# A recurrence, a routed feed-forward layer and a mish layer on one core: another PSUM bank for k's rows, weights loaded in parts, alpha's range checked elsewhere

## The chip, the core and the metric

The kernel runs on one core of a Trainium2 chip. Its time is the device time of one execution in microseconds (us); the number compared is the median of several executions. The engines are named as in the profile: PE (matrix multiply), PEld (its weight load), DVE (vector), ACT (activation), POOL (general purpose), SP (which here only issues DMAs). PE's clock has two levels, 1.2 and 2.4 GHz; the profile gives the granted clock as a share of the upper one, so 0.50 is the lower level all the time.

## The reference, cut to what matters

Four sequences (B = 4) of 8 heads, 768 steps and 48 columns go through a gated linear recurrence; its output, 3072 tokens of 384, goes to one of 8 experts each, and then through a dense layer with the mish function:

```python
for t in range(S):                                   # recurrence, per batch and head
    state = alpha[:, :, t, :, None] * state + np.einsum('bhd,bhe->bhde', k[:, :, t], v[:, :, t])
    y[:, :, t] = np.einsum('bhd,bhde->bhe', q[:, :, t], state)
expert_idx = np.argmax(x @ w_gate, axis=1)           # router: one expert a token
out[mask] = gate_w[mask, None] * (np.maximum(x[mask] @ w1[e], 0.0) @ w2[e])
g = h * np.tanh(np.log1p(np.exp(np.minimum(h, 20.0))))   # h = x @ w_in
return g @ w_out
```

## The kernel before, in words

The program is one order of instructions for each engine, written out by hand. It has three stages.

**Recurrence and routing.** A sequence of 768 steps is cut into 6 chunks of 128. Heads are taken in pairs (16 pairs in all), and two pairs make a round. One *unit* is one chunk of two pairs; there are 48 (`UNITS`). `run` (line 275) walks over them. In unit u it issues `scores(u+1)` (PE products of k and q into the PSUM tile `sc`, masked by DVE on line 223), `state(u)` (line 245, the chunk's contribution to the state, then DVE line 250 and ACT line 252), some of the setup, `rows_of_k(u+1)` (PE transposes on line 232 into `kps`, copied by ACT on line 234 into `kn`, which `state(u+1)` needs), the router's `step(2u)`, loads of v, more setup, `step(2u+1)`, and `result(u)` (line 264 and 269 into the PSUM tile `y`, copied by ACT on line 272). `kps` is the upper half of `y`'s first bank (line 82). `result` leaves a closure behind in `now`; the next `step(2u)` runs it: it turns y back into rows with PE (line 481, into the PSUM tile `xps`) and copies them with ACT (line 484).

**Setup** prepares k and q for a round of two pairs: PE transposes alpha, k and q (`columns`, line 118, PSUM tile `tp` with two buffers), ACT copies alpha's columns (lines 135 and 136), DVE scans them backward and forward (lines 152 and 169) and multiplies (line 181). `top` (line 138) checks alpha's range with two ACT passes over its rows, and only then loads the next alpha into the same tile. The first round is set up by halves of 384 steps, all later ones whole. The setup steps are in a list `todo`, each with a weight; `upto` runs them when they are due: the first 30 by unit 5, the rest by unit `READY` = 35. `busy` issues PE products of zeros to no purpose but to keep PE at work: 20 ahead of the first scores, 40 in units 1 and 3.

**Routing** (`Router`) makes each token's expert and place in small steps in a list `later`; below `SINGLE` = 76 half-units one of them runs per unit, after that several. `quick` (line 655) turns the range check into a flag.

**Experts** (lines 971 to 1006), with PE at work throughout, and beside them `fills`: DVE and ACT steps that narrow 64-bit weights to 32 bits, spread evenly over 116 slots. The weights of expert 0 come by two 1.5 MB DMAs on ACT's queue at half-unit 62, expert 1's first by one at 86; `pieces(0)` splits them from half-unit 72 on. **The mish layer** follows.

Of the kernel before, what the change touches and what calls it, by code (L numbers as in the profile page):

```python
# [21 lines left out]
P = 128  # L22
# [7 lines left out]
UNITS, READY = B * NC * NP // 2, 35  # L30

WARM_FIRST = 20
WARM, WARM_UNITS = 40, (1, 3)


class Attention:


    def __init__(self, ctx, early, late, tc, q, k, v, alpha, ident, warm, emit_y, place):
# [19 lines left out]
        self.rows = [tiles[:2], tiles[4:6], tiles[6:]]  # L59
        for n in range(2):  # L60
            for i in range(3):
                (nc.gpsimd if n else nc.vector).memset(self.rows[i][n][:, :, :, D:], 0.0 if i else 1.0)

# [8 lines left out]
        self.most = setup.tile([P, 1], F32, name="most")  # L72
        nc.gpsimd.memset(self.most, -A_MAX)
# [8 lines left out]
        self.kps = self.y[:, 0, 2 * P:].rearrange("p (j t) -> p j t", j=2)[:, :, :112]  # L82
        self.xps = ps_c.tile([P, 2, P], F32, name="xps")
# [10 lines left out]
        self.over = c.tile([P, 2, B * NP], F32, name="over")  # L94
# [6 lines left out]
    def load(self, i, n):  # L101

        if n < B * NP:
            t, b, hp = self.rows[i][n % 2], n // NP, n % NP
            for h in range(2):
                self.nc.sync.dma_start(out=t[:, :, h, :D],  # L106
                                       in_=self.src[i][b, 2 * hp + h].rearrange("(c p) d -> p c d", p=P))
# [7 lines left out]
    def columns(self, i, n, half):  # L115
        ps = self.ps_t.tile([P, 3, P], F32, name="tp")
        for j in range(3):
            self.nc.tensor.transpose(  # L118
                ps[:112, j], self.rows[i][n % 2][:, 3 * half + j].rearrange("p h d -> p (h d)")[:, :112], self.ident)
        if half and i:  # L120
            self.load(i, n + 2)
        return ps[:112]

    def alpha(self, n, half):
# [6 lines left out]
        if n == 0 and half:  # L131
            nc.vector.tensor_copy(to[:, :, 1:], ps[:, :, 1:])
            nc.vector.tensor_copy(self.a0[:, n % 2, cs], ps[:, :, 0])
        else:
            nc.scalar.activation(out=to[:, :, 1:], in_=ps[:, :, 1:], func=AF.Copy)  # L135
            nc.scalar.activation(out=self.a0[:, n % 2, cs], in_=ps[:, :, 0], func=AF.Copy)
# [48 lines left out]
    def setup(self):  # L185

        A = lambda n: [(0.3, lambda z=z: self.alpha(n, z)) for z in range(2)]
        top = lambda n: [(0.2, lambda: self.top(n))]
# [4 lines left out]
        lo, hi = (0, 384), (384, S)  # L193
        first = [*A(0), *back(0, *lo), *A(1), *back(1, *lo), *mid(0, 0, 3), *scale(1, 0, 0), *forth(0, *lo),
                 *scale(2, 0, 0), *forth(1, *lo), *scale(1, 1, 0), *scale(2, 1, 0)]
        rest = [*back(0, *hi), *back(1, *hi), *mid(0, 3, NC), *forth(0, *hi), *scale(1, 0, 1), *top(0),
                *scale(2, 0, 1), *forth(1, *hi), *scale(1, 1, 1), *top(1), *scale(2, 1, 1)]
        for p in range(2, B * NP, 2):
            q = p + 1
            rest += [*A(p), *back(p), *top(p), *A(q), *back(q), *top(q), *mid(p), *forth(p), *scale(1, p),  # L200
                     *forth(q), *scale(2, p), *scale(1, q), *scale(2, q)]
# [24 lines left out]
    def rows_of_k(self, u):  # L226
        nc = self.nc
        b, c, z, ns, t = self.pairs(u)
        if c < NC - 1:
            ps = self.kps  # L230
            for j, n in enumerate(ns):
                nc.tensor.transpose(ps[:, j], self.kh[n][:, t], self.ident[:112, :112])
            self.kn[u] = kn = self.wk.tile([P, 2, P], F32, name="kn")
            nc.scalar.activation(out=kn[:, :, :112], in_=ps, func=AF.Copy)
# [40 lines left out]
    def run(self, step):  # L275
# [5 lines left out]
        early, late = sum(w for w, _ in self.todo[:30]), sum(w for w, _ in self.todo[30:])  # L281
        due = lambda u: early * (u + 1) / 5 if u < 5 else early + late * (u - 4) / (READY - 5)
# [20 lines left out]
        for i in range(3):  # L303
            self.load(i, 0)
            self.load(i, 1)
        self.load_v(0)
        self.load_v(1)
        for n, (_, f) in enumerate(first):
            f()
            if n == 6:  # L310
                step(-4)
        loaded = 2
        self.busy(WARM_FIRST)
        scores(0)
        self.rows_of_k(0)
        for u in range(UNITS):
            if u + 1 < UNITS:
# [5 lines left out]
            step(2 * u)  # L323
# [9 lines left out]
            step(2 * u, True)  # L333
            step(2 * u + 1, True)
# [77 lines left out]
class Router:  # L412
# [14 lines left out]
    def setup(self, att, w_gate):  # L427
# [11 lines left out]
        self.bad = cst.tile([P, 2], BF16, name="bad")  # L439
        self.limits = cst.tile([1, NE + 2], F32, name="limits")  # L440
# [33 lines left out]
    def emit_y(self, b, c, z, yt):  # L474
# [157 lines left out]

    def step(self, second):

        if second:
            self.put(True)
            return
        if self.later:
            self.later.pop(0)()
        while self.now:  # L640
# [775 lines left out]
```

## Time and profile before

| | us |
|---|---|
| median of 3 runs | 927.88 (923.14 to 929.74) |
| profiled execution, its own time | 931.71 |
| its span, first to last instruction | 930.0 |
| PE / PEld / DVE / ACT / POOL busy in the span | 868.6 / 806.8 / 637.6 / 600.7 / 106.7 |

The profile is one execution. Busy time is summed over the span; a PE that is busy can still run at the lower clock, so a stage has to be read with the granted clock beside it. A wait is named by the waiting engine, its tile and line, and then by what released it; idle time of an engine off the path that sets the end costs nothing.

### The profile page before, as it was taken

What the parts mean: (1) busy time and instruction counts of PE and PEld (TensorE: products, weight loads), DVE (VectorE), ACT (ScalarE), POOL (GpSimd) and SP (SyncE); (2) the same over time, 40 slices, a digit from 0 to 9 for tenths busy, and PEclk for the clock granted to TensorE, in tenths of its full rate; (3) what the DMA queues carried; (4) which work ended last, traced back from release to release, by engine and by line L of the source; (5) the groups of instructions that cost most, each with busy time, mean ns of one, the idle gap of its engine ahead of it and who ended that gap; (6) DMA issues with size and microseconds to landing.
All of it is one profiled execution on the core that took longest, in us unless ns stands there. A gap on an engine that the chain in (4) does not pass through costs nothing.

```text
span 930.0 us, 15412 instructions
## 1 busy us (share of the span) xinstructions
PE 868.6 (93%) x5696; PEld 806.8 (87%) x5697; DVE 637.6 (69%) x1369; ACT 600.7 (65%) x1325; POOL 106.7 (11%) x162
## 2 busy tenths in 40 slices
PE   6889888798989999999999999999999999999993
PEld 4667666566779999999999899999999999999993
DVE  5556767455347877677663897868697777768682
ACT  1544565344335655455445998979797988889891
POOL 3000030204033101111003001010100101010101
PEclk8797999785589999999999999999999999999997
DMA  9843697662226667775652200000000000000000
GB/s 134 125 80 66 114 133 131 83 201 61 85 53 201 219 199 210 223 234 185 219 191 70 69 1 26 1 26 1 18 9 1 26 1 26 1 26 1 26 1 30
DMA packets 136877, 81.53 MB, mean 88 GB/s; under 512 B 111200, under 2 KB 126818, under 8 KB 136792
## 3 DMA queue, kind: packets, MB, share of 16 engines
q1 hardware_dynamic: 126632, 63.68, 28.9%
q0 software_dynamic: 4352, 9.41, 3.2%
q10 hardware_dynamic: 5808, 7.35, 2.5%
q8 instruction: 47, 0.77, 0.4%
q14 instruction: 38, 0.31, 0.1%
HBM read 66.79 MB, written 14.37 MB: 87 GB/s over the span
## 4 chain that ended last, share of the span: by engine, by line
PE 77%; issue 9%; ACT 5%; DVE 3%; DMA 3%; POOL 1%; SPq 1%; another core or an unknown queue 1%; POOLq 0%; ACTq 0%; DVEq 0%
PE o L1101 19%; PE hps L1057 19%; PE hps L981 12%; PE yps L1001 12%; PE tp L118 3%; PE y L264 2%; PE sc L220 2%; PE y L269 2%; ACT out L142 1%; PE xps L481 1%; SPq L106 1%; ACT at L135 1%; PE xtp L958 1%; ACT t L252 1%; POOL ids_dram L366 1%
## 5 line engine op out<-in xcount | busy, mean ns | idle before, releaser
L981 PE MATMUL hps<-xt,h 128*128 128x432 f32 x384 | 107.6, 358 | 0.0
L1064 DVE TENSOR_SCALAR u<-u 128x384 f32<-128x384 f32 x128 | 46.2, 361 | 83.1 <-ACT u L1063 80.2
L1071 ACT ACTIVATE r<-v,one 128x384 f32<-128x384 f32 x128 | 79.1, 618 | 4.2
L1072 ACT ACTIVATE r<-r,ln 128x384 f32<-128x384 f32 x128 | 79.0, 617 | 4.2
L981 PEld LDWEIGHTS hps<-xt,h 128*128 128x128 f32 x384 | 72.2, 188 | 3.4 <-ACT xt L968 0.2
L1080 DVE SCALAR_TENSOR_TENSOR u<-u,hps 128x384 f32<-128x384 f32 x128 | 70.9, 554 | 4.4
L923 DVE TENSOR_TENSOR l<-raw,h 128x512 fp32r<-128x512 f32 x96 | 64.8, 683 | 11.3 <-ACT h L921 11.3
L1063 ACT ACTIVATE u<-hps 128x384 f32<-128x384 f32 x128 | 61.2, 478 | 17.4 <-PE hps L1057 16.9
L1088 DVE TENSOR_TENSOR gl<-u,gh 128x384 fp32r<-128x384 f32 x128 | 70.6, 551 | 0.7 <-ACT gh L1084 0.6
L1077 DVE SCALAR_TENSOR_TENSOR u<-v,r 128x384 f32<-128x384 f32 x128 | 70.6, 551 | 0.0
L1079 DVE SCALAR_TENSOR_TENSOR u<-u,r 128x384 f32<-128x384 f32 x128 | 70.5, 551 | 0.0
L981 PE MATMUL hps<-xt,l 128*128 128x432 f32 x192 | 69.2, 361 | 0.0
L1001 PE MATMUL yps<-hh,h 128*128 128x432 f32 x192 | 69.1, 360 | 0.0
L1001 PE MATMUL yps<-hh,l 128*128 128x432 f32 x192 | 68.5, 357 | 0.0
L1001 PE MATMUL yps<-hlo,h 128*128 128x432 f32 x192 | 68.5, 357 | 0.0
L366 POOL DMA_INDIRECT out_dram<-xg,ix x24 | 23.4, 977 | 387.3 <-ACT xg L1115 382.4
L1070 ACT ACTIVATE v<-u 128x384 f32<-128x384 f32 x128 | 66.9, 522 | 1.6 <-DVE u L1064 0.2
L1084 ACT ACTIVATE gh<-u 128x384 fp32r<-128x384 f32 x128 | 65.8, 514 | 1.8 <-DVE u L1080 1.8
L1057 PE MATMUL hps<-x2h,winh 128*128 128x384 f32 x192 | 64.8, 337 | 2.0 <-DVE u L1080 2.0
L1101 PE MATMUL o<-raw,gh 128*128 128x384 f32 x192 | 65.2, 340 | 0.0
L1057 PE MATMUL hps<-x2h,winl 128*128 128x384 f32 x192 | 65.2, 340 | 0.0
L1101 PE MATMUL o<-h,gh 128*128 128x384 f32 x192 | 65.1, 339 | 0.0
(198 smaller groups left out, 2214.0 us busy)
## 6 DMA issues: line engine op xcount, KB each, us to landing
raw<-in_moe_w_dram SPq DMA_DIRECT2D x12, 1536.0 KB
raw<-in_moe_w_dram ACTq DMA_DIRECT2D x4, 1536.0 KB
f<-in_moe_w_out_dram SPq DMA_DIRECT2D x16, 384.0 KB
f<-in_moe_w_in_dram SPq DMA_DIRECT2D x10, 512.0 KB
h<-in_alpha_dram SPq DMA_DIRECT2D x32, 144.0 KB
l<-in_k_dram SPq DMA_DIRECT2D x32, 144.0 KB
l<-in_q_dram SPq DMA_DIRECT2D x32, 144.0 KB
vt<-in_v_dram SPq DMA_DIRECT2D x32, 144.0 KB
```

The source lines that it names most:

```text
L981: nc.tensor.matmul(ps, lhsT=a[:, k, f * P:f * P + P], rhs=x[:, k], start=n == 0, stop=n == 8)
L1001: nc.tensor.matmul(ps, lhsT=a[:, f, k * P:k * P + P], rhs=h[:, f], start=n == 0, stop=n == 23)
L1057: nc.tensor.matmul(ps, lhsT=a[:, k, fs], rhs=x[:, k], start=n == 0, stop=n == 8)
L1070: nc.scalar.activation(out=v, in_=self.u[g], func=AF.Square)
L1071: nc.scalar.activation(out=r, in_=v, func=AF.Ln, bias=self.one)
L1072: nc.scalar.activation(out=r, in_=r, func=AF.Exp, scale=-1.0, bias=self.ln2)
L1077: op(out=u, in0=v, scalar=1.0, in1=r, op0=ALU.add, op1=ALU.mult)
L1079: op(out=u, in0=u, scalar=4.0, in1=r, op0=ALU.subtract, op1=ALU.mult)
L1080: op(out=u, in0=u, scalar=2.0, in1=h, op0=ALU.add, op1=ALU.mult)
L1084: self.nc.scalar.activation(out=self.gg[g][0], in_=self.u[g], func=AF.Copy)
L1088: self.nc.vector.tensor_sub(gl, self.u.pop(g), gh.bitcast(F32))
L1101: nc.tensor.matmul(self.acc[i], lhsT=a[:, t], rhs=w, start=f == 0 and n == 0, stop=f == 15 and n == 2)
```

## The change

- `kps` moves from `y`'s bank to the bank of `xps` (one tile of four quarters). The copy of `kps` is split off as `keep_k`, and the order becomes: transposes of k, PE products of the way back into `xps`, ACT copy of `kps`, ACT copy of `xps`.
- `step(2u)` moves to the head of the unit, ahead of `scores(u+1)`; the way back no longer runs in it.
- `top` goes. Alpha gets four row tiles in place of two, and the next alpha is loaded as soon as PE has transposed the old one. A new class `Range` reads alpha a second time beside the experts: 18 DMAs of 128 x 512, 18 DVE maxima, and one small product at the end.
- Rounds 1 and 2 (pairs 2 to 5) are set up by halves too, and the halves are interleaved. The first 11 steps of `todo` are due by unit 2, the rest by unit 36.
- `busy(20)` stands ahead of the last two steps of the first half round; five times 20 in units 0 to 4 take the place of twice 40.
- k's first loads go on ACT's queue. Expert 0's weights come in 10 parts on SP's queue from half-unit 56 on, one a half-unit; expert 1's first in 6 parts from 82 on.
- Four zero fills of `xg` move from POOL at the start to ACT at half-units 76 to 79; the splitting of expert 0's weights starts at 74.

```diff
-UNITS, READY = B * NC * NP // 2, 35
+UNITS, READY = B * NC * NP // 2, 36
-WARM, WARM_UNITS = 40, (1, 3)
+WARM, WARM_UNITS = 20, range(5)
...
-        self.rows = [tiles[:2], tiles[4:6], tiles[6:]]
+        self.rows = [tiles[:4], tiles[4:6], tiles[6:]]
...
-        self.kps = self.y[:, 0, 2 * P:].rearrange("p (j t) -> p j t", j=2)[:, :, :112]
-        self.xps = ps_c.tile([P, 2, P], F32, name="xps")
+        out = ps_c.tile([P, 4, P], F32, name="xps")
+        self.xps, self.kps = out[:, :2], out[:, 2:, :112]
...
-        if half and i:
-            self.load(i, n + 2)
+        if half:
+            self.load(i, n + len(self.rows[i]))
...
-    def top(self, n):
-        for z in range(2):
-            t = self.wk.tile([P, NC * 2, D], F32, name="out", bufs=1)
-            self.nc.scalar.activation(out=t, in_=self.rows[0][n % 2].rearrange("p c h d -> p (c h) d")[:, :, :D],
-                                      func=AF.Relu, scale=1.0 - 2 * z, bias=self.most,
-                                      accum_out=self.over[:, z, n:n + 1])
-        self.load(0, n + 2)
...
+        first, rest = half(0, 0), half(0, 1)
+        first.insert(9, (0.0, lambda: self.busy(WARM_FIRST)))
+        for p in (2, 4):
+            rest += [*half(p, 0), *half(p, 1)]
...
-        early, late = sum(w for w, _ in self.todo[:30]), sum(w for w, _ in self.todo[30:])
-        due = lambda u: early * (u + 1) / 5 if u < 5 else early + late * (u - 4) / (READY - 5)
+        early, late = sum(w for w, _ in self.todo[:11]), sum(w for w, _ in self.todo[11:])
+        due = lambda u: early * (u + 1) / 2 if u < 2 else early + late * (u - 1) / (READY - 2)
...
-            self.load(i, 0)
-            self.load(i, 1)
+            for n in range(2):
+                self.load(i, n, self.nc.scalar if i == 1 else None)
...
         for u in range(UNITS):
+            step(2 * u)
             if u + 1 < UNITS:
                 scores(u + 1)
             self.state(u)
             upto(u + 0.3)
             if u + 1 < UNITS:
                 self.rows_of_k(u + 1)
-            step(2 * u)
+            back(lambda: u + 1 < UNITS and self.keep_k(u + 1))
...
-        def back():
+        def back(between):
             for j in range(2):
                 nc.tensor.matmul(ps[:, j], lhsT=yt[:, j], rhs=self.back[:, 2 * z + j], start=True, stop=True)
+            between()
...
+        def load(n):
+            self.rows[n] = t = self.p.tile([P, self.w], F32, name="alpha")
+            self.nc.sync.dma_start(out=t, in_=self.src[:, n * self.w:n * self.w + self.w])
+
+        def look(n):
+            self.nc.vector.tensor_reduce(out=self.most[:, n:n + 1], in_=self.rows.pop(n), op=ALU.max,
+                                         axis=mybir.AxisListType.X, apply_absolute_value=True)
...
-            if i == 62:
-                ex.load(0, 0, nc.scalar)
-                ex.load(0, 1, nc.scalar)
-            if i == 72:
+            if i == 56:
+                loads.extend(ex.load_parts(0, 0))
+                loads.extend(ex.load_parts(0, 1, 4))
+            if loads:
+                loads.pop(0)()
+            if i == 74:
...
-            if i == 86:
-                ex.load(1, 0, nc.scalar)
+            if i == 82:
+                loads.extend(ex.load_parts(1, 0))
...
+        rg = Range(words, tc, alpha)
+        for n, f in enumerate(rg.steps()):
+            fills.insert(3 + 4 * n, f)
```

## Rows read from the trace of the kernel before

**Rows 1.** Windows: stretch and length (us), busy per engine (count), clock, DMA share, GB/s
```profile
5.00:15.00 10.00, 4.68 (x29) 3.58 (x28) 7.62 (x15) 1.54 (x6) 4.97 (x39) 0.82 1.49 169
16.80:47.40 30.60, 25.30 (x245) 20.61 (x244) 18.56 (x32) 13.95 (x43) 0.00 (x0) 0.75 0.77 120
66.00:80.00 14.00, 14.00 (x95) 11.22 (x91) 6.99 (x14) 3.23 (x10) 0.00 (x0) 0.51 0.28 55
80.00:171.00 91.00, 78.09 (x898) 60.74 (x898) 66.50 (x133) 49.59 (x161) 11.89 (x21) 1.00 0.69 115
171.00:192.40 21.40, 15.20 (x105) 11.60 (x103) 9.43 (x18) 11.11 (x34) 3.56 (x4) 0.60 0.77 162
207.00:253.50 46.50, 40.74 (x305) 31.49 (x305) 21.38 (x89) 17.01 (x52) 12.08 (x17) 0.53 0.29 79
274.70:508.30 233.60, 233.60 (x1238) 223.71 (x1237) 161.01 (x299) 124.98 (x245) 38.99 (x36) 1.00 0.62 194
```

**Rows 2.** Windows of line 223 alone, one a unit: DVE busy (count), clock, DMA
```profile
66.00:80.00 14.00, 1.38 (x2) 0.51 0.28 55
80.00:171.00 91.00, 13.71 (x20) 1.00 0.69 115
207.00:253.50 46.50, 5.51 (x8) 0.53 0.29 79
```

**Rows 3.** Waits of PE, 0 to 275 us: total us, times, longest us
```profile
PE y L264 <- ACT kn L234: 22.6, 19, 5.7
...
PE tp L118 <- DMA h<-in_alpha_dram: 2.2, 2, 1.8
...
PE tp L118 <- ACT out L142: 1.5, 1, 1.5
...
PE route L536 <- DVE new L250: 0.8, 2, 0.6
```

**Rows 4.** Waits of PE, 80 to 171 us
```profile
PE y L264 <- ACT kn L234: 10.9, 11, 1.3
```

**Rows 5.** Waits of PE, 47.4 to 66 us
```profile
PE y L264 <- ACT kn L234: 3.1, 3, 1.6
```

**Rows 6.** Timeline inside one unit: start, us, engine, line, tiles, idle before
```profile
104.17 0.36 PE L232 MATMUL y<-ident,kh 112*128 112x112 f32 x2
...
105.46 0.37 ACT L234 ACTIVATE kn<-y 128x224 f32<-128x224 f32 x1
...
105.70 0.40 ACT L484 ACTIVATE x<-xps 128x240 f32<-128x240 f32 x1
...
105.89 0.65 PE L264 MATMUL y<-st,vt 128*64 128x128 f32 x8 [0.91 <-ACT kn L234]
```

**Rows 7.** Groups by line, 0 to 270 us: busy us, mean ns, idle before
```profile
L142 ACT ACTIVATE out<-h,most 128x576 f32<-128x576 f32 x32 | 24.7, 771 | 0.5
```

**Rows 8.** Timeline of the start
```profile
3.11 3.18 SPq L106 DMA_DIRECT2D l<-in_k_dram  x4
...
14.50 2.34 PE L207 MATMUL route<-warm 128*128 128x128 bf16 x20
...
14.76 0.55 DVE L181 TENSOR_TENSOR qh<-tp,scanf 112x384 f32<-112x384 f32 x1
...
16.77 1.23 PE L220 MATMUL sc<-qh,kh 48*128 48x128 f32 x8
```

**Rows 9.** Waits of SP's queue, 0 to 275 us
```profile
SPq L106 <- PE tp L118: 37.7, 20, 5.6
```

**Rows 10.** Line 907 (whole weight loads): issue ns min/median/max, first and last us
```profile
L907 SPq DMA_DIRECT2D raw<-in_moe_w_dram x12: 379/417/576, 303.5 to 465.3; - x12
```

**Rows 11.** Groups by line, 0 to 270 us: the two reductions nearest to `look`
```profile
L662 DVE TENSOR_REDUCE am<-acs 112x1 f32<-112x96 f32 x1 | 0.2, 243 | 0.0
...
L661 DVE TENSOR_REDUCE am<-over 128x1 f32<-128x32 f32 x1 | 0.2, 185 | 0.0
```

**Rows 12.** Waits, 275 to 508 us
```profile
ACT f64t L391 <- DMA f<-in_moe_w_in_dram: 15.8, 5, 4.7
```

More of the change, by code (lines that the diff above doesn't have):

```diff
@@ L62, in __init__ @@
                 (nc.gpsimd if n else nc.vector).memset(self.rows[i][n][:, :, :, D:], 0.0 if i else 1.0)
+        for n in (2, 3):
+            nc.gpsimd.memset(self.rows[0][n][:, :, :, D:], 1.0)
         self.at = [setup.tile([112, S + 1], F32, name=f"at{n}") for n in range(2)]
@@ L185, in setup @@
     def setup(self):
-        A = lambda n: [(0.3, lambda z=z: self.alpha(n, z)) for z in range(2)]
-        top = lambda n: [(0.2, lambda: self.top(n))]
+        A = lambda n, *hs: [(0.3, lambda z=z: self.alpha(n, z)) for z in hs or range(2)]
         back = lambda n, *s: [(1.0 if s else 1.8, lambda: self.back(n, *s))]
@@ L273, in result, with run @@
         self.emit_y(b, c, z, yt)
-    def run(self, step):
+    def run(self, step, back):
         self.units = [(b, c, z) for b in range(B - 1) for z in range(2) for c in range(NC)]
@@ L332, in run @@
             upto(u + 0.999)
-            step(2 * u, True)
-            step(2 * u + 1, True)
+            step(2 * u, after=True)
+            step(2 * u + 1, after=True)
 NE = 8
@@ L631, in release, with way_back @@
         self.held = None
+    def way_back(self, between=None):
+        if self.now:
+            self.now.pop(0)(between or (lambda: None))
+            assert not self.now
+        elif between:
+            between()
     def step(self, second):
@@ L636, in step, with some @@
             self.put(True)
-            return
-        if self.later:
+        elif self.later:
             self.later.pop(0)()
-        while self.now:
-            self.now.pop(0)()
-    def some(self, n, now=True):
-        while now and self.now:
-            self.now.pop(0)()
+    def some(self, n):
         first = True
@@ L729, in finish @@
         late = self.late
-        while self.now:
-            self.now.pop(0)()
+        self.way_back()
         while self.later:
@@ L740, in finish, with __init__, steps, all @@
         self.begins()
+class Range:
+    PARTS = 18
+    def __init__(self, ctx, tc, alpha):
+        self.nc = nc = tc.nc
+        pool = lambda name, bufs: ctx.enter_context(tc.tile_pool(name=name, bufs=bufs))
+        cst, self.p = pool("g_c", 1), pool("g_p", 2)
+        self.src = alpha.rearrange("b h s d -> (b h s d)").rearrange("(p n) -> p n", p=P)
+        self.w = B * H * S * D // P // self.PARTS
+        self.most = cst.tile([P, self.PARTS], F32, name="most")
+        self.bad = cst.tile([P, 1], BF16, name="above")
+        self.ones = cst.tile([P, 1], BF16, name="one_b")
+        nc.vector.memset(self.ones, 1.0)
+        self.rows = {}
+    def steps(self):
+        def load(n):
[4 more added lines that the diff above has]
+                                         axis=mybir.AxisListType.X, apply_absolute_value=True)
+        def all():
+            nc, m = self.nc, self.p.tile([P, 1], F32, name="m")
+            nc.vector.tensor_reduce(out=m, in_=self.most, op=ALU.max, axis=mybir.AxisListType.X)
+            nc.vector.tensor_scalar(out=self.bad, in0=m, scalar1=A_MAX, scalar2=None, op0=ALU.is_gt)
+        s = [lambda: load(0)]
+        for n in range(self.PARTS):
+            if n + 1 < self.PARTS:
+                s.append(lambda n=n: load(n + 1))
+            s.append(lambda n=n: look(n))
+        return s + [all]
+    def end(self, ps, flag, over):
+        nc = self.nc
+        nc.tensor.matmul(ps, lhsT=self.ones, rhs=self.bad, start=True, stop=True)
+        nc.vector.tensor_scalar(out=over[:, NE:NE + 1], in0=ps, scalar1=0.5, scalar2=None, op0=ALU.is_gt)
+        nc.vector.tensor_reduce(out=flag, in_=over, op=ALU.max, axis=mybir.AxisListType.X)
 class Late:
@@ L908, in load, with load_parts, part @@
         self.got[i] = t
+    def load_parts(self, e, i, many=6):
+        src = self.w[i][e].rearrange("(k p) f -> p k f", p=P)
+        def part(n):
+            if n == 0:
+                self.got[i] = self.raw.tile([P, 3072], F32, name=f"raw{i}")
+            t = self.got[i].rearrange("p (k f) -> p k f", k=src.shape[1])
+            w = src.shape[2] * src.shape[1] // many
+            k, f = divmod(n * w, src.shape[2])
+            if w < src.shape[2]:
+                self.nc.sync.dma_start(out=t[:, k, f:f + w], in_=src[:, k, f:f + w])
+            else:
+                ks = slice(k, k + w // src.shape[2])
+                self.nc.sync.dma_start(out=t[:, ks], in_=src[:, ks])
+        return [lambda n=n: part(n) for n in range(many)]
     def pieces(self, i, eng=None):
@@ L1196, in gla_moe_mish_kernel @@
         nc.gpsimd.memset(none, B * S)
-        for t in ex.xg:
-            nc.gpsimd.memset(t, 0.0)
-        work, due = [], [None]
+        work, loads, due = [], [], [None]
         def step(i, after=False):
@@ L1203, in step @@
                 if i >= SINGLE:
-                    ro.some(AFTER, False)
+                    ro.some(AFTER)
                 return
@@ L1238, in step @@
                 ro.late.open(ex, ident)
-        att.run(step)
+        att.run(step, ro.way_back)
         ro.finish()
@@ L1336, in gla_moe_mish_kernel @@
                 assert not fills
+                rg.end(ex.ps_t.tile([P, CAP], F32, name="xtp")[:1, :1], flag, over)
                 words.close()
```

61 lines of the change are left out of this document (30 added, 31 removed).

## The prediction, made before the changed kernel ran

> **What bounds the kernel now.** I read the busy time by stage with the granted clock beside it first. In the expert stage PE is busy 233.60 of 233.60 us at clock 1.00; the mish layer after it is PE work in the same way, and the change touches neither's products. So what can be won lies before 274.7 us, in the recurrence. There PE has two different troubles [rows 1, 2]. From 80 to 171 us the clock is 1.00; 20 units take 91.00 us, 4.55 each, of which PE works 78.09 / 20 = 3.9 and idles 12.9 in all. From 66 to 80 us PE is busy all 14.00 us, but at clock 0.51: two units take 7.0 each. A unit at the lower clock thus costs 7.0 / 3.9 = 1.8 times its work. The same clock holds from 207 to 253.5 us (0.53, eight units of 5.8), and for about half of 16.8 to 47.4 us (0.75 is the mean of 0.5 and 1.0, so 15.3 of 30.6 us).
>
> Then I read what PE waits for. One wait stands out: line 264, the products into `y`, for ACT's copy of `kn`: 22.6 us in 19 waits, the longest 5.7 [rows 3]; from 80 to 171 us it is 10.9 of the 12.9 idle [rows 4]. The timeline of one unit shows why. PE wrote k's rows into `y`'s bank at 104.17; ACT came to copy them only at 105.46, and line 264, whose own operands have nothing to do with `kn`, started at 105.89, once that copy was through [rows 6]. It waits for the bank, not for data. ACT comes late because it has the range check among other things: 32 passes of 771 ns, 24.7 us [rows 7].
>
> **The change part by part.** I sum against the profiled execution, 931.7 us (span 930.0 and 1.7 around it).
>
> *The bank.* `y` no longer waits for the copy of `kn`. Who waits instead? `state(u+1)` needs `kn`, but after `y`'s sixteen products (two lines of eight, 0.65 us each), some transposes and eight scores, over 2 us behind the transposes of k; the copy ended at 105.83, 1.7 us behind their start [rows 6]. So the copy is hidden by about half a unit, more with the range passes gone. PE's next writes to the new bank come a unit later, while ACT's copy of `xps` in that bank ended at 106.10 [rows 6], so they are not held either. What would be lost if the cover went is the same 0.9 us a unit.
>
> The Trainium skill speaks against this move: "PSUM — Partial Sum Buffer", section "PSUM bank collisions raise a hardware error", asks to guard PSUM by bank and quadrant and not by address, so the new neighbours in one bank hold each other up as the old ones did. The trace agrees that a bank is guarded as a whole. By the rule alone the wait would only change its name, and this term would be nothing; that is the second rival below.
>
> Of the 22.6 us I leave out the one wait of 5.7 (a stall at 171 us in which ACT stood still too) and have 16.9 us. The bounds are 0 and 16.9. DVE is the next candidate: 66.50 / 20 = 3.3 us a unit [rows 1, 2], so at 4.0 us a unit it would be busy 83%, not the bound, but in order and with long scans. I take two thirds: **-11.3**.
>
> *The clock from 66 to 80 us.* The fall came behind three waits of this kind, 3.1 us in 18.6, the longest 1.6 [rows 5]. Without them I expect PE to keep the clock: two units of 3.9 instead of 14.00 us, **-6.2** (bounds 0 and -6.2).
>
> *The first units.* With four alpha tiles and the range passes gone, PE no longer waits for alpha (1.8) and for ACT's pass ahead of it (1.5) [rows 3]: -3.3. The second round's setup is spread out instead of crowded into five units. Lower-clock time of 15.3 us costs 15.3 x (1 - 3.9 / 7.0) = 6.8 us more than its work; I take half of it back, -3.4 (bounds 0 and -6.8). There are 20 more idle products, 100 for 80: at 2.34 / 20 = 0.117 us each [rows 8] up to 2.3 us; half of it, as the upper clock makes them shorter, +1.2. Together **-5.5**.
>
> *The start.* The 20 idle products ran from 14.50 to 16.84 and scores began at 16.77, although the last operand was ready at 14.76 + 0.55 = 15.31 [rows 8]. Ahead of the last two steps they fill a wait; scores follow the operand: **-1.4**. k's loads on ACT's queue let SP issue q up to 3.18 us sooner [rows 8], but from 5 to 15 us the DMA engines are full (share 1.49) [rows 1], so I take nothing for it, bounds 0 and -3.2. The Trainium skill says the same ("DMA: Bandwidth & Descriptors", section "Issuing engines are not separate DMA queues": only the sequencer's issue time is saved); by it this would be 0 as well, and the trace's full share agrees.
>
> *Routing ahead of scores.* The routing step's PE products now stand in front of scores and state. Their waits for DVE are at most 0.6 us, 0.8 in two [rows 3]; nine such groups give 0 to +5.4. Their operands are made a step earlier, so I take **+1**.
>
> *Alpha's range beside the experts.* 18 loads of 128 x 512 x 4 bytes = 0.26 MB, and 18 reductions. From 185 ns for 32 elements and 243 for 96 [rows 11], 0.9 ns an element, a reduction of 512 is estimated at 0.62 us: 11 us of DVE in a stage where it is busy 161.01 of 233.60 us [rows 1]. PE hides it. ACT waits in that stage already for loads up to 4.7 us [rows 12] and PE shows none of it. I take **+1**; the upper bound is the last rival.
>
> *At nothing.* The weights in parts: 16 issues on SP in place of three on ACT, 16 x 0.417 = 6.7 us [rows 10], spread over 16 half-units, behind which k, q, alpha and v are queued; SP has 37.7 us of waiting for PE in this stage [rows 9], which covers it, and without the cover up to 6.7 us of loads would be late. The `xg` fills: four ACT passes of at most 0.77 us [rows 7] where ACT is busy 17.01 of 46.50 us [rows 1]. The halves add 8 scans and 10 small DVE steps; at 0.55 us each (a product, [rows 8]) under 10 us of DVE, inside its 24.5 idle from 80 to 171 us alone [rows 1].
>
> *The rest.* From 171 to 192.4 us (a stall, then clock 0.60) and from 207 to 253.5 us I change nothing: at the lower clock PE is busy 40.74 of 46.50 us there [rows 1] and nothing in the change takes PE work away.
>
> Sum: -11.3 - 6.2 - 5.5 - 1.4 + 1 + 1 = -22.4; 931.7 - 22.4 = 909.3. The profiled execution lies 3.8 us above the median of the runs (927.9), so the forecast for the median is 905.5, say **906**, with its own range 896 to 916.
>
> **The rivals.**
>
> *The last units keep the clock too.* Eight units from 207 us would take 40.74 / 1.8 = 22.6 us of PE work and the 5.8 idle, 28.4 instead of 46.5: 18 us more, **888**. For it: a denser PE earlier on fell less. Against it: the clock stayed at 0.53 there with PE busy 88% [rows 1]. Chance 0.20.
>
> *The bank only gets another partner.* PE waits for ACT's copy of `xps` or `kn` in the new bank: the terms -11.3 and -6.2 are gone, 906 + 17.5 = **923**, no measurable change. For it: banks are guarded whole [rows 6]. Against it: a full unit lies between. Chance 0.15.
>
> *DVE takes the wait over.* It is at 73% [rows 1] and the halves add to it; half of both terms is lost, 906 + 8.8 = **915**. Chance 0.10.
>
> *Slower: the range check reaches PE in the expert stage.* A part is 0.26 MB at 194 GB/s [rows 1], 1.35 us, ahead of the weight words on SP's queue, and 0.62 us of DVE. If nothing covers it, 18 x 1.97 = 35 us: **941**. It decides from 23 us on, 1.3 us a part. For it: ACT's waits for those words, 15.8 us in five [rows 12], show that DMA is close. Against it: PE is busy all the time in spite of them. Chance 0.12.
>
> **How the numbers follow.** Forecast 0.43, and 0.20, 0.15, 0.10, 0.12 as above. A measurement here can tell about 1% from no change, 9.3 us: below 918.6 is faster, above 937.2 slower. Faster: 0.43 + 0.20 + 0.10 = 0.73; same 0.15; slower 0.12. The range 886 to 923 takes in the forecast, both clock cases and the lost bank; outside are the slower rival and the outer edge of the others, about 2 in 10.
>
> **What would show it.** Right: PE's wait of `y` for `kn` gone and no wait of line 232 or 481 for ACT in its place; clock 1.00 through 60 to 80 us; 80-to-171-like units at about 4.0 us; the expert stage still 233 to 235 us. Wrong: waits of PE for `xps`, DVE above 90%, gaps of PE among the experts, or v's and q's transposes waiting for loads while the weight parts are under way. If the lower clock comes and goes at other places than I assume, the sum can miss by 6 to 18 us in either direction with every other step right.

## The result and the profile after

Four executions of the changed kernel have a median of 897.27 us (891.42 to 900.63), beside 925.51 us for the kernel before on the same chip: the ratio is 0.973, 95% interval 0.968 to 0.977. It is faster by 25 us by that ratio; the forecast was 906, with 896 to 916 as its own range. The profiled execution took 895.0 us, its span 892.9, which is 37 us less than the profiled execution of before. The medians lie 28 us apart and the ratio stands for 25, so 9 to 12 of these 37 are the choice of executions: that of before lay above its median and this one below. One kernel's executions differ by up to 2.6%, and stretches at the lower clock stand at other places from profile to profile; ratios below carry their interval for that reason.

First the busy time by stage. The columns are the stretch and its length in us, then busy time and count of PE, PEld, DVE, ACT and POOL, the granted clock, the DMA share and GB/s. The first row is everything ahead of the experts' first product, for before:

```profile
0.00:274.70 274.70, 229.80 (x2156) 178.83 (x2158) 161.60 (x391) 120.89 (x380) 44.29 (x102) 0.81 0.58 107
```

and the same stretch and some of its stages, then the expert stage, for the changed kernel:

```profile
0.00:237.40 237.40, 215.56 (x2177) 167.87 (x2178) 160.38 (x405) 96.78 (x322) 44.58 (x100) 0.86 0.73 124
18.00:62.00 44.00, 43.72 (x548) 36.00 (x548) 34.38 (x75) 17.88 (x64) 0.00 (x0) 1.00 0.77 119
61.90:145.00 83.10, 75.48 (x862) 58.57 (x860) 67.37 (x140) 37.78 (x134) 13.03 (x20) 1.00 0.81 141
176.20:233.30 57.10, 55.36 (x399) 42.79 (x398) 26.24 (x115) 23.77 (x71) 16.16 (x17) 0.50 0.36 76
237.50:471.20 233.70, 233.70 (x1237) 223.28 (x1237) 172.48 (x322) 124.35 (x245) 41.28 (x36) 1.00 0.68 214
```

The experts begin at 237.4 instead of 274.7 us, 37.3 us sooner, and the expert stage is as long as before (233.70 for 233.60, [rows 1]) although DVE does 11.5 us more in it. So all of the gain lies in the recurrence. Two things make it up. PE's idle time there (length less busy time) falls from 274.7 - 229.8 = 44.9 to 237.4 - 215.6 = 21.8 us: 23.1. The rest, 14.2, is PE's own busy time, which is shorter because less of it runs at the lower clock: the mean of 0.81 stands for 2 x 0.19 x 274.7 = 104 us at the lower level, 0.86 for 66. From 18 to 62 us, where the mean clock of before is 0.84, it is now 1.00.

The waits of PE ahead of the experts (engine, tile and line; what released it; us in total, times, longest):

```profile
PE tp L117 <- DVE qh L167: 3.3, 4, 1.7
PE tp L117 <- POOL pre L461: 2.7, 1, 2.7
PE sc L211 <- DVE st L214: 2.5, 6, 0.6
PE route L239 <- DMA vt<-in_v_dram: 2.2, 3, 1.8
PE xps L479 <- ACT yt L266: 2.2, 5, 0.9
...
PE route L239 <- ACT kn L228: 0.5, 2, 0.3
```

The 22.6 us of `y` for `kn` [rows 3] are gone, and `kn` itself costs 0.5 where it is really needed. What is left is small, and most of it a wait for DVE. One new wait stands at the start: alpha's transposes, 2.7 us up to 9.35. The row names POOL's fill, which ended at 9.28, but the same transposes wait for alpha's fourth load too, and its last part landed at 9.21; in e1 and e10, where the fill was done by 8.53, the wait is 2.4 us and for that load alone. In before this load landed at 6.53. It is issued at 2.52 us in both kernels; what differs beside it are k's loads, now on ACT's queue.

Where the 37.3 us were won is best read along the units. DVE's masking of the scores occurs once a unit; from the starts of these 48 instructions come the lengths below, in us. The later rows are experiments, told of in the next section.

| kernel | to unit 0 | 0 to 5 | 5 to 11 | 11 to 29 | 29 to 35 | 35 to 47 | 47 to experts | PE idle in all |
|---|---|---|---|---|---|---|---|---|
| before | 18.1 | 31.2 | 33.0 | 79.1 | 36.2 | 59.9 | 17.3 | 44.9 |
| changed | 17.3 | 20.6 | 23.9 | 75.4 | 24.2 | 60.5 | 15.4 | 21.8 |
| e1, changed, old bank | 17.6 | 22.3 | 25.1 | 84.5 | 27.2 | 53.0 | 17.6 | 36.3 |
| e2, before, new bank | 18.3 | 31.0 | 25.2 | 77.2 | 34.2 | 57.9 | 18.6 | 28.4 |
| e3, before, no passes | 18.1 | 27.3 | 29.1 | 80.5 | 33.8 | 58.2 | 17.2 | 36.4 |
| e4, changed, passes back | 17.8 | 22.0 | 25.7 | 92.9 | 27.1 | 57.0 | 18.0 | 31.8 |
| e9, before, bank and no passes | 18.0 | 26.8 | 24.3 | 73.1 | 36.0 | 55.0 | 14.9 | 23.6 |
| e6, changed, whole weights | 17.5 | 22.2 | 23.9 | 75.5 | 36.6 | 59.2 | 18.4 | 29.0 |
| e7, changed, whole rounds | 17.6 | 24.5 | 24.7 | 68.2 | 30.6 | 55.9 | 18.0 | 24.1 |
| e8, changed, old idle products | 19.1 | 22.9 | 22.8 | 75.5 | 27.9 | 62.1 | 15.6 | 21.8 |
| e5, changed, v earlier | 18.0 | 23.3 | 23.9 | 75.5 | 26.1 | 51.5 | 15.8 | 25.9 |
| e10, changed, scatters spread | 17.6 | 22.2 | 23.9 | 75.4 | 24.4 | 57.8 | 18.1 | 26.7 |
| e11, e10 with v earlier | 17.9 | 20.6 | 23.9 | 75.4 | 24.2 | 54.2 | 15.6 | 21.4 |
| e12, e11 with idle products | 17.6 | 22.2 | 23.9 | 75.4 | 24.4 | 49.7 | 18.1 | 23.4 |

Between the first two rows the change won 0.8, 10.6, 9.1, 3.7, 12.0, -0.6 and 1.9 us. A row is one execution. The 12.0 us in units 29 to 35 were forecast as nothing, and in units 11 to 29, where most of the bank's 11.3 us were expected, only 3.7 appeared.

### The profile page after: what moved, and what is told of

It reads as the page before. It is cut to its first block, busy times and chain, and to the rows that moved or that the text cites. A ratio compares the mean times of both kernels' runs of the same rounds, so it can differ in the third digit from the quotient of the medians.

```text
span 892.9 us, 15497 instructions
## 1 busy us (share of the span) xinstructions
PE 854.7 (96%) x5717; PEld 795.7 (89%) x5718; DVE 648.2 (73%) x1406; ACT 576.3 (65%) x1267; POOL 109.3 (12%) x160
## 4 chain that ended last, share of the span: by engine, by line
PE 79%; DVE 9%; issue 6%; ACT 3%; POOL 1%; DMA 0%; SPq 0%; POOLq 0%; ACTq 0%; DVEq 0%
PE o L1163 20%; PE hps L1119 20%; PE hps L1043 13%; PE yps L1063 13%; PE tp L117 2%; PE y L258 2%; PE sc L211 2%; DVE scanf L155 2%; PE y L263 2%; PE xps L479 2%; DVE scanb L138 2%; DVE st L214 1%; ACT at L130 1%; PE xtp L1020 1%; PE route L198 1%
## 5 line engine op out<-in xcount | busy, mean ns | idle before, releaser
L1125 ACT ACTIVATE u<-hps 128x384 f32<-128x384 f32 x128 | 61.3, 479 | 17.3 <-PE hps L1119 16.9
L363 POOL DMA_INDIRECT out_dram<-xg,ix x24 | 23.4, 977 | 387.3 <-ACT xg L1177 382.5
```

## The experiments: bank and range passes

**e1: the bank undone.** The changed kernel, with k's rows in `y`'s bank again.

```diff
-        out = ps_c.tile([P, 4, P], F32, name="xps")
-        self.xps, self.kps = out[:, :2], out[:, 2:, :112]
+        self.kps = self.y[:, 0, 2 * P:].rearrange("p (j t) -> p j t", j=2)[:, :, :112]
+        self.xps = ps_c.tile([P, 2, P], F32, name="xps")
```

> The changed kernel with one thing undone: k's rows stand in y's bank again. Theory 1 (the bank is the main gain): y waits for kn again, 10 us or more in sum, and the time is 907 to 915. Theory 2 (ACT is early enough once the 32 range passes are gone, so the bank matters little): the waits come back with less than 5 us in sum, 897 to 902.

Measured: 914.21 us, ratio 0.984 (0.970 to 0.998). The row of PE's waits:

```profile
PE y L258 <- ACT kn L228: 15.0, 16, 2.2
```

The wait is back, without ACT's range passes too, and PE idles 36.3 us, 14.5 more than with the new bank: theory 1. The wait decides and not the time, as this interval reaches into that of the changed kernel (0.968 to 0.977). The profiled execution, the shortest of five (span 902.8), had less time at the lower clock than that of the changed kernel (clock 0.91 to the experts), which hides a part of the 14.5 in its length.

**e2: the bank alone, in the kernel before.** The same move in the other direction; the copy of k's rows is issued behind the products of the way back.

```diff
-        self.kps = self.y[:, 0, 2 * P:].rearrange("p (j t) -> p j t", j=2)[:, :, :112]
-        self.xps = ps_c.tile([P, 2, P], F32, name="xps")
+        out = ps_c.tile([P, 4, P], F32, name="xps")
+        self.xps, self.kps = out[:, :2], out[:, 2:, :112]
...
                 self.rows_of_k(u + 1)
+            back(lambda: u + 1 < UNITS and self.keep_k(u + 1))
```

> The kernel before with the bank alone moved: k's rows beside xps, their copy issued behind the products of the way back. Theory 1: 909 to 915, the wait of y for kn (22.6 us) is gone. Theory 2, and the rival by which the wait only gets another partner: 922 to 928, and PE waits for ACT at xps or at k's transposes instead.

Measured: 917.90 us, ratio 0.980 (0.962 to 0.999); that is 910 on the first median of before, theory 1. All waits of PE that have to do with the new bank, ahead of the experts:

```profile
PE xps L486 <- ACT yt L275: 2.4, 3, 1.7
...
PE xps L486 <- issue: 0.5, 1, 0.5
...
PE route L248 <- ACT kn L237: 0.2, 1, 0.2
```

No wait of PE for a copy out of the shared bank took the old one's place: 22.6 us went, and 0.2 us came for `kn`. The wait for `yt`, the way back's own operand, rose from 0.5 to 2.4. PE idles 28.4 us, 16.5 less than before. Units 5 to 11 show the lower clock of 66 to 80 us gone (33.0 to 25.2), by the bank alone, and units 0 to 5 show nothing (31.2 to 31.0). This profile is of the longest of four executions (919.57 us), and its later lower-clock time is not used; e9 below bears out what is read from it, as there PE idles 12.8 us less than in e3 and the clock is 1.00 from 42 to 138 us.

**e3: the kernel before without the range passes.** Alpha's range is not looked at; the loads stay.

```diff
     def top(self, n):
-        for z in range(2):
-            t = self.wk.tile([P, NC * 2, D], F32, name="out", bufs=1)
-            self.nc.scalar.activation(out=t, in_=self.rows[0][n % 2]..., func=AF.Relu, ...)
         self.load(0, n + 2)
```

> The kernel before without the 32 ACT passes of alpha's range check (the check is left out; the loads stay where they were). Theory 1: ACT comes a little sooner to the copies, 3 to 8 us: 918 to 924. Theory 2: most of the gain is here already, 905 to 913.

Measured: 921.50 us, ratio 0.992 (0.987 to 0.996), theory 1.

```profile
PE y L260 <- ACT kn L230: 14.4, 15, 2.1
PE y L260 <- issue: 4.4, 1, 4.4
```

With 24.7 us of ACT work gone, PE still waits 14.4 us for the copy behind the shared bank. Each kernel has one wait beside these that comes with a stall, 5.7 us in before and 4.4 here (the second row); without it, 16.9 us stand against 14.4. So ACT's load made these waits a little longer, and the shared bank is why they are there. PE idles 8.5 us less. Units 0 to 5 gain 3.9 us.

**e4: the range passes put back into the changed kernel,** with the load of the next alpha behind them as before.

```diff
-            return [*A(p, z), *back(p, *s), *A(q, z), *back(q, *s), *mid(p, *m),
+            return [*A(p, z), *back(p, *s), *top(p), *A(q, z), *back(q, *s), *top(q), *mid(p, *m),
...
-            rest += [*A(p), *back(p), *A(q), *back(q), *mid
+            rest += [*A(p), *back(p), *top(p), *A(q), *back(q), *top(q), *mid
```

> The changed kernel with the 32 ACT passes put back beside the setup (the next alpha is loaded behind them again, into four tiles). Theory 1: nothing that PE waits for depends on ACT by so much any more, 897 to 902. Theory 2: the 24.7 us of ACT work cost 8 us or more, 905 to 915.

Measured: 924.81 us, ratio 0.998 (0.993 to 1.003): nearly the whole gain is gone, so theory 1 is wrong here, and the cost is above theory 2's range. In the row of PE's waits, the products of the way back wait for ACT's copy of `y`, their own operand:

```profile
PE xps L493 <- ACT yt L280: 11.1, 10, 2.6
```

That is not the old wait under another name (it isn't for the bank), but the same late ACT. PE idles 10.0 us more than in the changed kernel, and the lower clock makes PE's busy time 13.1 longer (228.7 for 215.6). Why e2, with the same passes, waits only 2.4 us at this place was not settled.

**e9: both parts in the kernel before.** The edits of e2 and e3 together (the range is not looked at).

> The kernel before with two parts of the change: k's rows in the other bank, and no ACT passes for alpha's range (the range check is left out). Theory 1 (these two carry the change; PE's idle time before the experts falls by 16 + 9 = 25 us of 44.9): idle 17 to 24 us, ratio 0.968 to 0.980. Theory 2 (halves, warm-up and weights in parts carry a good share): ratio 0.982 to 0.990.

Measured: 902.96 us, ratio 0.976 (0.970 to 0.982), theory 1; by its time this kernel can't be told from the changed one (0.973). The stretch to the experts:

```profile
0.00:248.10 248.10, 224.49 (x2156) 174.66 (x2157) 161.70 (x390) 94.47 (x316) 46.65 (x103) 0.83 0.69 119
```

PE's idle time falls by 44.9 - (248.1 - 224.5) = 21.3 of the 23.1 us that the whole change wins. The bank is worth 16.5 us of idle with the passes in place and 36.4 - 23.6 = 12.8 without them; the passes 8.5 and 4.8. What the profile of e9 lacks against that of the changed kernel stands in two columns of the table: 6.2 us in units 0 to 5, and 11.8 in units 29 to 35; in units 11 to 29 and 35 to 47 e9 is the shorter, by 2.3 and 5.5.

## The experiments: the rest of the change

**e6: expert 0's and 1's weights as whole loads on ACT's queue,** at half-units 62 and 86, as before.

```diff
-            if i == 56:
-                loads.extend(ex.load_parts(0, 0))
-                loads.extend(ex.load_parts(0, 1, 4))
-            if loads:
-                loads.pop(0)()
+            if i == 62:
+                ex.load(0, 0, nc.scalar)
+                ex.load(0, 1, nc.scalar)
...
-                loads.extend(ex.load_parts(1, 0))
+                ex.load(1, 0, nc.scalar)
```

> The changed kernel with expert 0's weights in two whole loads on ACT's queue at half-unit 62 and expert 1's in one at 86, as before. Theory 1 (the parts are what removed the stall at 171 us and the lower clock behind it): a stall of 4 us or more of PE between 140 and 180 us and the lower clock behind it, ratio 0.983 to 0.992. Theory 2 (the parts were costed at nothing): ratio 0.968 to 0.977.

Measured: 911.80 us, ratio 0.979 (0.970 to 0.987), between the two forecasts; the profile decides. From its timeline (start and duration in us, engine, line, operation, tiles, count, and idle time before it with its releaser; ACTq is ACT's sequencer issuing DMAs):

```profile
152.42 11.50 ACTq L951 DMA_DIRECT2D raw<-in_moe_w_dram  x2
...
163.97 0.56 ACT L246 ACTIVATE t<-new,acs 112x48 f32<-112x48 f32 x2 [11.19 <-DMA raw<-in_moe_w_dram]
164.82 0.40 PE L239 MATMUL route<-vt,kn 128*48 128x48 f32 x4 [3.83 <-ACT kn L228]
```

The first row sums up two issues. Each of them took 0.37 us (the three numbers are the shortest, the middle and the longest issue in ns):

```profile
L951 ACTq DMA_DIRECT2D raw<-in_moe_w_dram x2: 374/376/378, 152.4 to 163.5; - x2
```

Between them ACT stood still. The second waits for a semaphore, the same that tells of the landing of one of v's loads, which SP had issued at 149.85; by the trace's semaphore events that load's last part landed at 163.53, and the second issue began at 163.55. So an older transfer held ACT and not the issue itself. PE then waited 3.8 us for the copy of k's rows, and units 29 to 35 take 36.6 us instead of 24.2; a PE wait of 2.1 us at 150.6 and a stretch at the lower clock from 152.1 to 158.9 come ahead of the hold, so not all of the 12.4 are its doing. By the medians e6 lies 0.006 of the ratio above the changed kernel, and the intervals overlap.

All five profiles with whole loads on ACT have 33.8 to 36.6 us in these units (before, e2, e3, e6, e9), the nine with parts 24.2 to 30.6. But the cause isn't one. In e9 ACT stood for 4.8 us in the same way: the first issue began at 163.70, behind the landing at 163.68 of a store that SP had issued at 152.98, and PE waited 4.3 us for ACT. In e2 the two issues came 0.02 us behind two such landings, and ACT stood for 1.5 us. In before and e3 the semaphores had been free for 7 us or longer, the issues (0.44 to 0.49 us each) held nothing, and a stall stands some 6 to 9 us ahead of them. e2 has such a stall too.

**e7: rounds 1 and 2 set up whole,** with due times as before.

```diff
-UNITS, READY = B * NC * NP // 2, 36
+UNITS, READY = B * NC * NP // 2, 35
...
-        for p in (2, 4):
-            rest += [*half(p, 0), *half(p, 1)]
-        for p in range(6, B * NP, 2):
+        for p in range(2, B * NP, 2):
...
-        early, late = sum(w for w, _ in self.todo[:11]), sum(w for w, _ in self.todo[11:])
-        due = lambda u: early * (u + 1) / 2 if u < 2 else early + late * (u - 1) / (READY - 2)
+        early, late = sum(w for w, _ in self.todo[:28]), sum(w for w, _ in self.todo[28:])
+        due = lambda u: early * (u + 1) / 5 if u < 5 else early + late * (u - 4) / (READY - 5)
```

> The changed kernel with rounds 1 and 2 set up whole and the due times as before. Theory 1 (halves and due times keep the clock up from 15 to 60 us): lower clock for 10 us or more in 15 to 80 us, ratio 0.980 to 0.990. Theory 2 (bank and range passes alone do it): ratio 0.968 to 0.977.

Measured: 901.25 us, ratio 0.969 (0.962 to 0.976), theory 2. The clock is 1.00 from the start to 150 us without the halves too:

```profile
0.00:150.00 150.00, 134.01 (x1493) 104.53 (x1494) 111.22 (x222) 58.65 (x210) 25.03 (x76) 1.00 0.87 135
```

They win at most 4 us in units 0 to 5 and lose 7 in units 11 to 29; a stall of 4.8 us of ACT at 148 us in e7 (units 29 to 35: 30.6 us for 24.2) hides that in its time. The middle of the recurrence, for the changed kernel:

```profile
61.90:137.30 75.40, 68.91 (x792) 53.57 (x792) 59.95 (x121) 34.58 (x123) 9.93 (x18) 1.00 0.85 144
```

and the same 18 units in e7:

```profile
66.90:135.10 68.20, 66.52 (x782) 52.44 (x781) 57.94 (x117) 33.83 (x121) 11.36 (x18) 1.00 0.77 128
```

PE idles 6.5 us in the one and 1.7 in the other, with work on every engine that differs by 2 to 4%, POOL's aside. DVE's backward scans wait for ACT's alpha copies in both, nine times in the changed kernel from 61.9 to 145 us and four times in e7:

```profile
DVE scanb L138 <- ACT at L130: 11.3, 9, 2.1
```
```profile
DVE scanb L138 <- ACT at L130: 5.9, 4, 1.5
```

So the halves and due times seem to leave the setup steps at worse places in the units, as DVE is busy 80% of the time and ACT 46% in the changed kernel; which of the two edits does it was not tried. A kernel with whole rounds and v earlier (below) was not tried.

**e8: idle products as before,** 20 ahead of the first scores and 40 in units 1 and 3.

```diff
-WARM, WARM_UNITS = 20, range(5)
+WARM, WARM_UNITS = 40, (1, 3)
...
-        first.insert(9, (0.0, lambda: self.busy(WARM_FIRST)))
...
+        self.busy(WARM_FIRST)
         scores(0)
```

> The changed kernel with the idle products as before: 20 ahead of the first scores, 40 in units 1 and 3. Theory 1 (the twenty more and their places hold the clock in the first units): start of unit 0 some 1 us later and lower clock for 5 us or more before 40 us, ratio 0.978 to 0.988. Theory 2 (they do nothing that the denser work doesn't do): ratio 0.970 to 0.976, from the start alone.

Measured: 902.21 us, ratio 0.970 (0.962 to 0.978), theory 2. Unit 0 starts 1.8 us later than in the changed kernel; units 0 to 5 take 22.9 us, within the 20.6 to 23.3 of the kernels with the new places, and the clock is 1.00 from 0 to 140 us.

## The experiments: the last units

In the changed kernel the clock is at 1.00 from 18 us to about 176 us and then at the lower level to 233 us. Two us before it fell, PE had waited for v, which is loaded one unit before its use there:

```profile
173.53 0.68 PE L239 MATMUL route<-vt,kn 128*48 128x48 f32 x4 [1.78 <-DMA vt<-in_v_dram]
```

**e5: v three units earlier.**

```diff
-            while loaded < min(B * NP, 6 + 2 * max(0, u // 6 - 1), 4 + int(spent / 7)):
+            while loaded < min(B * NP, 6 + 2 * max(0, (u + 3) // 6 - 1), 4 + int(spent / 7)):
```

> The changed kernel with v loaded three units sooner. Theory 1 (PE's late wait for v near 173 us, 1.8 us, starts the stretch at the lower clock that lasts to 233 us): the wait is gone, the clock holds for several units more, and the ratio to the kernel before falls from 0.973 to 0.950 to 0.965. Theory 2 (the last units leave PE too little work at the upper clock, whatever starts it): only the 1.8 us, ratio 0.968 to 0.974, lower clock from about 175 us again.

Measured: 895.12 us, ratio 0.961 (0.950 to 0.971), theory 1. The wait is gone, from 25 us on the clock holds to about 189 us but for two dips of 3.4 us (at 76 and 151), and units 35 to 47 take 51.5 us instead of 60.5. Two us before it fell this time, PE had waited for DVE, at a routing product:

```profile
186.88 0.17 PE L535 MATMUL route<-oh,tri 128*128 128x8 bf16 x1 [2.52 <-DVE new L244]
```

In e10, below, the fall at 180 us comes behind a wait of 2.4 us for v that ended at 178.4, in e11 that at 184 us behind the same wait for DVE as here, which ended at 181.9. The order of wait and fall is the same in these four, but it is no rule: in e8 the clock falls at 181.1 for 61 us with no PE wait of over 0.7 us in the 6 us ahead of it, and in e1 it stays at 1.00 behind a wait of 2.2 us that ended at 146.7. What the experiment shows is that with v earlier the fall comes later. In e5 a stall follows, in which ACT and DVE both stand:

```profile
188.61 0.65 PE L211 MATMUL sc<-qh,kh 48*128 48x128 f32 x4
...
190.56 0.97 POOL L363 DMA_INDIRECT ids_dram<-ids,pos  x1 [0.30 <-issue]
...
192.75 0.38 ACT L266 ACTIVATE yt<-y 112x256 f32<-112x256 f32 x1 [3.90 <-remote]
192.79 0.69 DVE L214 TENSOR_TENSOR st<-sc,mask 128x512 f32<-128x512 f32 x1 [3.38 <-remote]
193.19 0.57 PE L479 MATMUL xps<-back,yt 112*128 112x120 f32 x1 [2.88 <-ACT yt L266]
```

The profile has PE's products of their operands end by 189.8 us, but these ends are modelled, and the semaphore by which PE tells of them rose only at 192.67 and 192.76; so PE itself may have stood as well. Stalls of 2 to 5 us in which an engine waits for nothing that the profile shows of this core stand ahead of 230 us in before (at 171 and 225 us) and in e1 to e8, at most two in a profile, and each ends inside a batch of POOL's scatters or within 2 us behind it.

**e10: the scatters one a half-unit,** to take them out of the row, **and e11: the same with v earlier.**

```diff
-            for n in range(size):
-                scatter(self.tc, "ids", ...)
+            if size == 6:
+                self.spread += [lambda n=n: one(n) for n in range(size)]
...
+            if ro.spread:
+                ro.spread.pop(0)()
```

> The changed kernel with POOL's scatters of the tokens' places issued one a half-unit in the three batches of six, in place of six in a row. Theory 1 (the stalls of 2 to 5 us in which ACT, DVE and PE stand together come from six scatters in a row): no such stall before the experts, ratio 0.955 to 0.970. Theory 2 (scatters and stalls only fall into the same stretch of the program): a stall of 2 us or more somewhere in 90 to 215 us again, ratio 0.970 to 0.977.

> The changed kernel with the scatters spread and v loaded three units sooner. If stalls and the late v are what brings the lower clock on, it holds up to 190 us or longer and the experts start by 228 us: ratio 0.950 to 0.962. If the last units fall to the lower clock whatever comes before, the start lies at 232 to 238 us: ratio 0.964 to 0.974.

Measured: e10 902.10 us, ratio 0.977 (0.971 to 0.982); e11 892.08 us, 0.966 (0.960 to 0.972). e10 says nothing on the stalls. Its scatters ran 1.3 to 2.3 us apart in the first two batches, hardly otherwise than in the changed kernel (1.2 to 2.7): POOL depends on no product of those half-units and issues what it has. Neither e10 nor e11 shows a stall, but the changed kernel's profile shows none either. What e11 against e10 does show is v: 0.011 of the ratio, some 10 us, and on one chip their executions don't overlap (888.9 to 895.3 us against 897.5 to 903.7). e5 against the changed kernel gives 0.012, with intervals that overlap a little.

**e12: e11 with 12 idle products in each of units 38 to 43.**

```diff
+TAIL, TAIL_UNITS = 12, range(38, 44)
...
+            if u in TAIL_UNITS:
+                self.busy(TAIL)
```

> As the one before, with 12 idle products in each of units 38 to 43. Theory 1 (more products keep the clock up in the last units, as PE is idle there otherwise): clock 0.8 or more from 180 to 215 us, the experts start 5 us or more sooner than without them. Theory 2 (they only cost their own time, 72 of 0.06 to 0.12 us): the start is 2 to 8 us later than without them, the clock as it was.

Measured: 887.36 us (886.55 to 889.88), ratio 0.960 (0.954 to 0.965), the fastest median of all. The windows of 30 us, of e11

```profile
190.00:220.00 30.00, 29.77 (x220) 22.80 (x219) 10.58 (x50) 10.11 (x32) 4.43 (x5) 0.50 0.30 72
```

and of e12:

```profile
190.00:220.00 30.00, 27.82 (x327) 22.27 (x326) 15.69 (x75) 13.14 (x43) 6.79 (x9) 0.94 0.55 93
```

The clock is at the upper level, 0.94 for 0.50, and units 35 to 47 take 49.7 instead of 54.2 us. The experts start no sooner for it (231.4 for 231.7). Of the 4.5 us, 2.5 go between unit 47 and the experts, where PE now waits for the gather of the first expert's rows, and 1.6 in units 0 to 5, where e12 had 3.4 us at the lower clock ahead of any added product. So theory 1 is right on the clock and wrong on the gain: without those 1.6 us the start would be some 2 us sooner, not 5.

```profile
PE xtp L843 <- DMA xg<-x_dram,ix: 3.1, 3, 2.1
```

The step from e11 to e12 (0.966 to 0.960) is within their intervals.

## Why the prediction was right, and where it wasn't

The time and the order of causes came out: the gain lies ahead of the experts, the wait of `y` for `kn` is gone, nothing of it came back, and the expert stage didn't notice the range check. Against the profiled executions the sum (-22.4) is short by 14 us; against the ratio of the medians (-25 us) it is nearly right. Its terms did less well than their sum, and that the sum came so near is in part luck: two terms missed by 5 and 12 us, and in units 11 to 29 most of the bank's gain didn't show.

**The bank (-11.3, bounds 0 and -16.9).** In PE's idle time 16.5 us in e2, 14.5 in e1, 12.8 between e3 and e9: right, and near the far bound. In each of these edits k's rows change the program's tile together with the bank, so that it is the bank and not the tile that makes line 264 wait, as the prediction read from [rows 6], is not shown. The rival by which the bank only gets another partner fell; e2 shows 0.2 us in its place. It rested on the Trainium skill ("PSUM — Partial Sum Buffer", section "PSUM bank collisions raise a hardware error"). The rule to guard by bank is not contradicted: e1 and e3 show the wait as soon as `y` and `kps` share one. But beside `xps` sharing cost 0.2 us in e2 and 0.5 in the changed kernel: there the two uses lie half a unit apart.

**The clock from 66 to 80 us (-6.2).** Right: e2 gains 7.8 us in units 5 to 11 by the bank alone.

**The first units (-5.5).** Too small: 10.6 us. The bank has no part in it (e2), the passes 4 (e3, e9); the rest came with halves, due times and idle products. e8 undoes the last of these within the spread of 20.6 to 23.3 us among like kernels, e7 the first two with 24.5, 1.2 above it, so what each gives is not settled. All of the lower-clock time went, where I took half.

**The start (-1.4) and routing ahead of scores (+1).** Unit 0 came 0.8 us sooner. The prediction took nothing for k's loads on ACT's queue and put its bounds on the side of a gain; with them alpha's fourth load landed 2.7 us later than in before (9.21 for 6.53) and held the first transposes up. Waits at the routing products are 1.0 us in all; that step was not undone by itself.

**Alpha's range beside the experts (+1).** 0.1 us by the two expert stages; DVE's work there rose by 11.5 us, the estimate was 11. The slower rival fell.

**"At nothing. The weights in parts", and the stretch from 171 to 192.4 us.** This is the step that failed: 12.0 us went in units 29 to 35, where the sum has nothing. I costed what the parts add to SP's queue and overlooked what they take from ACT's: loads in ACT's order can make ACT wait for an older DMA, 11.2 us in e6, 4.8 in e9, 1.5 in e2. But that is not what the change took away from before, where the weights' issues at 183.3 held nothing. There the time was a stall of ACT that ended at 173.9 us, the wait of PE of 5.7 that came with it [rows 3] and that I had left out, and the lower clock from 175.3 to 192.3. Neither came in the changed kernel's execution; that the parts are the reason is not shown, and e7, which has the parts, has a stall of 4.8 us in the same units. On the issue of DMAs by several engines the prediction named the Trainium skill ("DMA: Bandwidth & Descriptors", section "Issuing engines are not separate DMA queues"), which calls an issue's time usually small beside the transfer. The trace agrees: 0.37 to 0.49 us for an issue of 1.5 MB of weights.

**"At nothing. The halves."** They add the DVE work that was counted, and cost 7 us in units 11 to 29 by their places (e7). That is where most of the bank's gain in these units went: 79.1 to 75.4 with the whole change, 68.2 with rounds whole. The rival of DVE taking the wait over named this half rightly (PE's waits are mostly for DVE now), but DVE's load isn't its cause: in e7 DVE is busy 85% of these units and PE idles less.

**The range passes (only 1.5 of the 3.3).** Under-sized: 4.8 to 8.5 us of idle in before, and in the changed kernel nearly the whole gain (e4). I counted the one wait that named line 142 and not the share of the passes in every late copy by ACT.

**The last units (0).** Right: 59.9 and 60.5 us. The rival's 18 us for a full clock there was too high a price: e12, at the upper level for most of these units, takes 49.7 us there, 10 less than before, and 0.8 more from unit 47 to the experts.

## What to carry to other kernels

A wait that names a copy may be for its bank: look whether the waiting instruction reads the copy at all, and then move the bank, but ask as well what else makes the copying engine late: with its range passes put back, ACT cost the changed kernel nearly all of its gain. When a DMA goes to or leaves an engine's queue, ask which older DMA its issue waits for, as that engine stands still so long (11.2 us of ACT in e6), and not only how long the issue takes. In a stage with two clock levels read idle time and lower-clock time apart: the bank's idle time agreed in three comparisons (12.8 to 16.5 us), the lower-clock time fell differently in each kernel.

## What was not expected of the hardware

Two DMA issues of 0.37 us each had ACT standing for 11.2 us in one kernel (e6), while in before they held nothing. In this program the DMAs that SP and ACT issue share eight semaphores, and in e6, e9 and e2 an issue on ACT came 0.02 us behind the landing of the older DMA on its semaphore; in e6 that was v's load, 13.7 us from issue to landing. In before the two semaphores had been free for 12 and 8 us. Why v's load took so long was not settled.

In some of the stalls a load of instructions is under way, and a long one. In e5 there is one between 187 and 194 us, whose packets fill 3.0% of 16 engines' 7 us, 3.4 us:

```profile
q8 instruction: 1, 0.02, 3.0%
```

In the changed kernel four of them from 102 to 140 us take 0.7% of 16 x 38 us, 1.1 us each:

```profile
q8 instruction: 4, 0.07, 0.7%
```

The Trainium skill ("Runtime: NRT & Kernel Launch", section "Instruction fetch mechanics") says that engines stream their instructions ahead and that the cost is mostly hidden. A late fetch beside POOL's scatters could explain the standstill of 3.9 us; that it is the cause is only argued, as e10 hardly moved the scatters in its first two batches and several of the stalls, both of before's among them, show no such load.
